# DeltaNet inverses: zeros above the diagonal written by GpSimd memsets, row and column factors in two bands

## The chip, the cores and the metric

The kernel runs on one core of a Trainium2 chip. The metric is the device time of one execution in microseconds, as the median of several runs. TensorE is called PE (its weight loads PEld), VectorE DVE, ScalarE ACT, GpSimd POOL and the queue of SyncE, which issues most transfers, SP.

## The reference

A linear-attention block (DeltaNet) feeds a mixture of experts. Batch 4, heads 8, sequence 768, head size 48; 3072 tokens of 384 numbers; 16 experts in 4 groups, hidden size 1024; everything in fp32.

```python
k_n = k / (np.linalg.norm(k, axis=-1, keepdims=True) + 1e-06)
for t in range(S):
    y[:, :, t] = q_t @ state
    v_old = state.T @ k_t
    state = state + beta_t * outer(k_t, v_t - v_old)
x = y.transpose(0, 2, 1, 3).reshape(B * S, H * D)
# one group by argmax, one expert in it by argmax, each token:
out = g_w * e_w * (relu(x @ w1[g, e]) @ w2[g, e])
```

(The middle lines are shortened to their meaning.)

## The kernel before

The sequence is cut into 24 chunks (u) of 32 steps. Inside a chunk the recurrence is a triangular system: with the products k·k of the chunk (gram, its products on line 253) and the factors beta/|k|^2 a unit lower triangular 32 x 32 matrix is inverted for every batch, head and chunk. Four chunks make a group (g, six of them). One group is 128 x 1024 numbers: on a partition lies one 32 x 32 matrix (tile m, 4 batches x 4 chunks x 8 heads = 128 matrices), and DVE inverts all 128 at once.

`inverse(g)` (from line 290 on) is that work. DVE turns the gram products into m (line 296). Square roots of the diagonal are made by DVE for group 0 and by POOL for the other groups (lines 307 to 312, 14 small steps on 128 x 32, result nrm); then r0 = -beta/|k|^2. Line 347 multiplies every row of m by its r0 (128 x 1024). Lines 355 to 383 run the elimination column by column, some 90 small DVE steps. Then line 386 builds cs, a table of -1 below the diagonal and 0 elsewhere (the constant `below`) times r0 by column, line 389 multiplies m by it, line 391 puts -r0 on the diagonal, and line 394 turns the result into mt. ACT spreads mt chunk by chunk into mtb (line 409, or 405 for the last group; each chunk two copies), the form that PE takes.

`advance(u)` is one chunk: PE adds vh (the values, scaled by DVE on line 435) and the old state's part into a_ps (lines 448, 454); ACT copies -a_ps to f (line 458); PE multiplies the inverse with it, w_ps from mtb and f (line 472); ACT copies w (line 475); PE updates the state s_ps (line 482), which ACT copies to s_bd (line 488); PE finishes the output o_ps (lines 496 or 501), which ACT copies to x (line 505). `logits(u)` turns x (t_ps, xt) and makes the router's logits (l_ps, lg); `route` does the routing per group partly on POOL, among it the comparisons `at` (line 602), whose products with `mine` PE adds up on line 684. Grams run ten chunks ahead.

The order of all engines in this stage is written out by hand. A loop over the chunks issues PE's and ACT's steps, and `work(n)` and `allow(...)` between them push the tasks that stand behind (the inverses, the routing): a task yields the size of each DVE step (or a word for what it waits for), `work` gives every task a credit and takes 100 plus that size from it per step:

```python
held[task] = said if isinstance(said, str) else None
due[task] -= 100 + (said if isinstance(said, int) else 0)
...
due[task] = min(due[task] + n * 180 * rate[task], 4000.0)
```

So the sizes that `inverse` yields decide between which steps of PE and ACT its own steps stand. The steps that it has on ACT (mtb) are issued when the task comes to ACT_STEP and SPREAD and the loop allows them. Each engine then runs its own list strictly in that order and waits by semaphores. After the attention the experts run one after the other, with weights of 3 MB each streamed in.

Constants (con) come in three loads: a small part, the table `below` (512 KB), and the rest. Before the first chunk PE multiplies columns of `below` by the identity into s_ps (line 787), products that nothing reads.

Of the kernel before, what the change touches and what calls it, by code (L numbers as in the profile page):

```python
# [8 lines left out]
F32 = mybir.dt.float32  # L9
I32 = mybir.dt.int32  # L10
AX = mybir.AxisListType
ALU = mybir.AluOpType
ACT = mybir.ActivationFunctionType
PSUM = bass.MemoryType.PSUM

C = 32
RG = 4
# [9 lines left out]
def constants(n_tokens, seq, n_experts, n_group, n_batch):  # L27
# [3 lines left out]
    p = np.arange(128)  # L31
    i, k = np.meshgrid(np.arange(C), np.arange(C), indexing="ij")
    u = np.arange(n_tokens // 128)
# [9 lines left out]
        "parity": np.stack([p // C % 2 == b2 for b2 in range(2)], axis=1),  # L43
        "below": np.tile(-(i > k).astype(np.float32).reshape(1, C * C), (128, 1)),
        "ident": (p[:, None] == p[None, :]),
# [13 lines left out]
    at, n = {}, 0  # L59
# [7 lines left out]
def deltanet_then_moe(  # L67
# [13 lines left out]
    nc = tc.nc  # L81
# [28 lines left out]
    con = cp.tile([128, const_d.shape[1]], F32, name="con")  # L110
    cut = {name: con[:, a:b] for name, (a, b) in const_at.items()}
    ident, before, ones = cut["ident"], cut["before"], cut["ones"]
# [64 lines left out]
    with ExitStack() as first:  # L177
# [21 lines left out]
        def load_kv(u):  # L199
            nc.sync.dma_start(out=kv_[u % NV], in_=kv_d[u])  # L200

        cols = [0, const_at["below"][0], const_at["ident"][0], const_d.shape[1]]

        def load_con(i):
            part = slice(cols[i], cols[i + 1])
            nc.sync.dma_start(out=con[:, part], in_=const_d[:, part])
# [13 lines left out]
        def of_kq(u, a=None):  # L220
            return (kqt_[u % NB][:, a or 0, 0], [lambda: load_kq(u, a)])
# [3 lines left out]
            RG: [of_kq(RG + 2), of_kq(RG + 3)],  # L225
            RG + 2: [of_kq(u, 1) for u in range(RG)] + [(cut["below"], [lambda: load_con(1)])],
            2 * RG: [(kv_[0], [lambda: load_kv(0), lambda: load_con(2), lambda: load_kv(1)])],
            2 * RG + 2: [of_kq(2 * RG), of_kq(2 * RG + 1)],
# [57 lines left out]
        def halves(g, uu):  # L286

            return range(1 if one_by_one(g, uu) else 2)

        def inverse(g):  # L290

# [4 lines left out]
            nc.vector.transpose(out=flat, in_=gts.pop(g).rearrange("p t u h -> p (t u h)"))  # L296
            yield C * C
            diag = flat[:, ::C + 1]
            nrm, r0, r1, r2 = [sm.tile([128, C], F32, tag=n, name=f"{n}{g}")
# [46 lines left out]
            yield FACTOR if g else 0  # L346
            nc.vector.tensor_tensor(m, m, r0[:, :, None].to_broadcast([128, C, C]), op=ALU.mult)  # L347
            yield C * C
            while g and g - 1 not in turned_over:
# [13 lines left out]
            for j in range(1, C - 1):  # L363
# [9 lines left out]
                else:  # L373
# [10 lines left out]
                    yield n * j  # L384
            cs = wk.tile([128, C, C], F32, tag="cs", name=f"cs{g}", bufs=1)
            nc.vector.tensor_tensor(cs, cut["below"].rearrange("p (i j) -> p i j", i=C),
                                    r0[:, None, :].to_broadcast([128, C, C]), op=ALU.mult)
            yield C * C
            nc.vector.tensor_tensor(m, m, cs, op=ALU.mult)
            yield C * C  # L390
            nc.vector.tensor_scalar(diag, r0, -1.0, None, op0=ALU.mult)
            yield
# [49 lines left out]
        def advance(u):  # L442
# [14 lines left out]
            f = wk.tile([128, H, D], F32, tag="f", name=f"f{u}")  # L457
            nc.scalar.activation(f, a_ps, ACT.Copy, scale=-1.0)
            o_ps = ps.tile([128, H, D], F32, tag="o", name=f"o_ps{u}")
# [295 lines left out]
        with tc.manual_schedule(engines={mybir.EngineType.PE, mybir.EngineType.DVE,  # L755
# [30 lines left out]
            for n in (H * D, H * D, H * D // 2):  # L786
                nc.tensor.matmul(s_ps[:, 0, 0:n], lhsT=ident, rhs=cut["below"][:, 0:n],
                                 start=True, stop=True, skip_group_check=True)
# [495 lines left out]
```

## Time and profile before

| | |
|---|---|
| median of the runs | 509.54 us (3 runs, 508.9 to 512.34) |
| profiled execution | 506.17 us, its span 504.4 us |
| granted TensorE clock, mean | 0.986 |
| PE busy | 465.6 us (92%) |
| DVE busy | 249.6 us (49%) |
| ACT busy | 187.3 us (37%) |
| POOL busy | 188.3 us (37%) |
| attention, up to the first expert product | 233.9 us of the span |

In the profile, "L347" is line 347. A row of a timeline has the start, the duration, engine, line, operation, output and inputs by the program's names, and in brackets the idle time of that engine just before and what ended it; `x32` means that many instructions merged, from the first start to the last end. Durations of neighbouring steps of one engine overlap by some 0.1 us, so a cost on the engine is better taken from start to start.

### The profile page before, as it was taken

Reading aid. Unit: us, or ns where it says so; the run is one execution under the profiler, and the core shown is the slowest. Engines: PE = TensorE matmul, PEld = TensorE weight load, DVE = VectorE, ACT = ScalarE, POOL = GpSimd, SP = SyncE. Lnnn points to the kernel's source line nnn. Section 1 sums busy time; section 2 is a strip of 40 time slices with the busy share of each in tenths; the row PEclk is TensorE's granted clock in tenths of the full one; section 3 lists DMA queues with packets and bytes.
Section 4 is the critical chain, followed back from the end, with each engine's and each line's share of the span. In section 5 each row is a group of like instructions: output and inputs, shape, how many; then the busy total and the mean of one; then the engine's idle time right before and its main releaser. Section 6 shows DMA issues by size and latency. Waiting matters only on the chain.

```text
span 504.4 us, 18596 instructions
## 1 busy us (share of the span) xinstructions
PE 465.6 (92%) x8012; PEld 428.2 (85%) x8012; DVE 249.6 (49%) x845; ACT 187.3 (37%) x396; POOL 188.3 (37%) x292
## 2 busy tenths in 40 slices
PE   3467999999999799899999999999999999999992
PEld 3345888878888688789999999999999999999992
DVE  2999999999999996528112012201201211012210
ACT  3224777677776667652121121112111111111110
POOL 0040110641715414010545454446525643356222
PEclk9997999999999999999999999999999999999997
DMA  5765445544435453221988779669868977789751
GB/s 181 228 223 167 142 152 172 156 134 155 146 104 168 139 170 109 71 64 36 289 279 275 254 223 302 221 202 324 269 190 276 323 270 218 245 298 303 229 182 40
DMA packets 57334, 99.98 MB, mean 198 GB/s; under 512 B 18974, under 2 KB 41433, under 8 KB 57251
## 3 DMA queue, kind: packets, MB, share of 16 engines
q1 hardware_dynamic: 51331, 88.77, 54.0%
q0 software_dynamic: 5920, 10.00, 6.5%
q8 instruction: 64, 1.05, 0.9%
q14 instruction: 19, 0.16, 0.1%
HBM read 84.63 MB, written 14.27 MB: 196 GB/s over the span
## 4 chain that ended last, share of the span: by engine, by line
PE 40%; DVE 29%; DMA 16%; issue 5%; POOL 4%; SPq 3%; ACT 2%; DVEq 0%; POOLq 0%; ACTq 0%
PE h_ps L1051 15%; PE y_ps L1070 14%; DMA y_dram<-yq 8%; DVE t L377 6%; DVE m L383 6%; DMA out_dram<-yo,to_i 5%; DVE m L360 4%; DMA yr<-y_dram 3%; SPq L1110 3%; PE w_ps L472 2%; DVE m L347 1%; DVE vh L435 1%; ACT s_bd L488 1%; DVE gqm L277 1%; PE x_ps L805 1%
## 5 line engine op out<-in xcount | busy, mean ns | idle before, releaser
L1070 PE MATMUL y_ps<-hid,w 128*128 128x224 f32 (+15 forms) x768 | 132.2, 332 | 0.0
L1070 PEld LDWEIGHTS y_ps<-hid,w 128*128 128x128 f32 x768 | 129.1, 190 | 0.3
L1051 PE MATMUL h_ps<-xt,w 128*128 128x232 f32 (+14 forms) x720 | 122.7, 330 | 0.0
L1051 PEld LDWEIGHTS h_ps<-xt,w 128*128 128x128 f32 x720 | 120.1, 190 | 0.3
L1023 POOL DMA_INDIRECT xq<-x_dram,from_q x92 | 87.6, 952 | 36.1 <-issue 24.7
L1054 ACT ACTIVATE hid<-h_ps 128x448 f32<-128x448 f32 (+15 forms) x64 | 32.1, 501 | 100.2 <-PE h_ps L1051 100.2
L1082 POOL DMA_INDIRECT out_dram<-yo,to_i x32 | 34.1, 1067 | 92.2 <-DVE yo L1120 82.3
L1073 DVE COPY yt<-y_ps 128x232 f32<-128x232 f32 (+13 forms) x14 | 5.1, 366 | 124.5 <-PE y_ps L1070 124.5
L1075 ACT ACTIVATE yt<-y_ps 128x224 f32<-128x224 f32 (+15 forms) x34 | 11.4, 336 | 116.6 <-PE y_ps L1070 116.6
L377 DVE TENSOR_TENSOR t<-m 128x81 f32<-128x81 f32 (+13 forms) x156 | 51.6, 331 | 0.2
L383 DVE TENSOR_TENSOR m<-m,t 128x81 f32<-128x81 f32 (+13 forms) x156 | 51.5, 330 | 0.0
L360 DVE SCALAR_TENSOR_TENSOR m<-m 128x29 f32<-128x29 f32 (+27 forms) x174 | 43.1, 251 | 0.4
L1120 DVE TENSOR_SCALAR yo<-yr,gate 128x384 f32<-128x384 f32 (+14 forms) x28 | 11.3, 422 | 61.4 <-DMA yr<-y_dram 51.6
L488 ACT ACTIVATE s_bd<-s_ps 48x768 f32<-48x768 f32 x46 | 37.0, 804 | 10.1 <-PE s_ps L482 9.5
L409 ACT ACTIVATE mtb<-mt,con 128x256 f32<-128x256 f32 x41 | 29.7, 737 | 4.2 <-DVE mt L394 4.2
L253 PE MATMUL g_ps<-kqt 48*32 48x64 f32 (+1 forms) x1216 | 18.4, 237 | 13.2 <-issue 8.5
L472 PE MATMUL w_ps<-f,mtb 64*64 64x48 f32 (+1 forms) x864 | 26.7, 217 | 2.5 <-ACT mtb L409 1.4
L472 PEld LDWEIGHTS w_ps<-f,mtb 64*64 64x64 f32 (+1 forms) x864 | 23.6, 128 | 5.8 <-issue 2.6
L454 PEld LDWEIGHTS a_ps<-s_bd,kqt 128*32 128x32 f32 x736 | 15.0, 110 | 15.9 <-ACT s_bd L488 7.2
L253 PEld LDWEIGHTS g_ps<-kqt 48*32 48x32 f32 x1216 | 14.4, 116 | 15.1 <-issue 9.4
L572 POOL TENSOR_TENSOR acc<-acc,hots 128x16 f32<-128x16 f32 x16 | 4.9, 307 | 57.3 <-DVE hots L570 56.3
L482 PE MATMUL s_ps<-w,kv 32*112 32x96 f32 x736 | 24.7, 272 | 0.0
(175 smaller groups left out, 589.2 us busy)
## 6 DMA issues: line engine op xcount, KB each, us to landing
w<-in_w_dram SPq DMA_DIRECT2D x29, 1536.0 KB, 12.1
kv<-in_kv_dram SPq DMA_DIRECT2D x24, 448.0 KB, 4.0
kqt<-in_kq_dram SPq DMA_DIRECT2D x20, 512.0 KB, 4.0
x_dram<-x SPq DMA_DIRECT2D x24, 192.0 KB, 2.1
w<-in_w_dram SPq DMA_DIRECT2D x24, 128.0 KB, 3.6
y_dram<-yq SPq DMA_DIRECT2D x36, 84.0 KB, 8.5
yr<-y_dram SPq DMA_DIRECT2D x14, 192.0 KB, 2.4
kqt<-in_kq_dram SPq DMA_DIRECT2D x8, 256.0 KB, 3.4
```

The source lines that it names most:

```text
L253: nc.tensor.matmul(g_out[quads[b], hh * NP + j, of], lhsT=kqt[rows, 0, j, quads[b]], rhs=kqt[rows, of, j, quads[b]], start=True, stop=True ...
L360: nc.vector.scalar_tensor_tensor(row, in0=m[:, j, 0:j], scalar=m[:, i, j:j + 1], in1=row, op0=ALU.mult, op1=ALU.add)
L377: nc.vector.tensor_tensor(tv, m[:, j + 2:, j:j + 1].to_broadcast([128, n, j]), m[:, j:j + 1, 0:j].to_broadcast([128, n, j]), op=ALU.mult)
L383: nc.vector.tensor_tensor(below, below, tv, op=ALU.add)
L409: nc.scalar.activation(mtb[:, rows, a], from_, ACT.Copy, scale=by)
L472: nc.tensor.matmul(w_ps[b, h], lhsT=mt[b, uu * H + (h % 2) * NP + h // 2], rhs=f[b, h], start=True, stop=True, skip_group_check=True)
L488: nc.scalar.activation(s_bd[rows, :, :, hh, :], s_at[rows, :, :, hh * D:(hh + 1) * D], ACT.Copy)
L1023: nc.gpsimd.indirect_dma_start(out=xq[:, g, :], out_offset=None, in_=x_dram[:, :].rearrange("n (q c) -> (n q) c", q=4), in_offset=bass.Ind ...
L1051: nc.tensor.matmul(h_ps[:, k], lhsT=w1[:, j, (f + k) * 128:(f + k + 1) * 128], rhs=xt[:, j, 0:R], start=(j == 0), stop=(j == DC - 1), skip ...
L1054: nc.scalar.activation(hid[:, f:f + 2], h_ps, ACT.Relu)
L1070: nc.tensor.matmul(y_ps, lhsT=w2[:, f, j * 128:(j + 1) * 128], rhs=hid[:, f], start=(f == 0), stop=(f == FC - 1))
L1082: put = nc.gpsimd.indirect_dma_start(out=out[:, :], out_offset=bass.IndirectOffsetOnAxis(ap=to[0:P, i:i + 1], axis=0), in_=yo[0:P, :], in_ ...
```

## The change

The constant `below` and its load go. Five memsets on POOL per group write zeros above the diagonal of m, right after DVE's turn: blocks of 16 x 16, then 2 of 8 x 8, 4 of 4 x 4, 8 of 2 x 2 and 16 single elements, slanted along the diagonal (496 elements per partition). The row factor is put on in two bands, rows 16 to 31 with all columns (512 elements) and rows 0 to 15 with columns 0 to 15 (256). The table cs is no longer built: m is multiplied by r0 by column in the same two bands, so without the -1 of `below`; the diagonal is a copy of r0 and not -r0, and f is a_ps instead of -a_ps, which takes the sign out. PE's unread products before the first chunk take columns of con from the identity on.

```diff
-        "below": np.tile(-(i > k).astype(np.float32).reshape(1, C * C), (128, 1)),
...
-        cols = [0, const_at["below"][0], const_at["ident"][0], const_d.shape[1]]
+        cols = [0, const_at["ident"][0], const_d.shape[1]]
...
-            RG + 2: [of_kq(u, 1) for u in range(RG)] + [(cut["below"], [lambda: load_con(1)])],
-            2 * RG: [(kv_[0], [lambda: load_kv(0), lambda: load_con(2), lambda: load_kv(1)])],
+            RG + 2: [of_kq(u, 1) for u in range(RG)],
+            2 * RG: [(kv_[0], [lambda: load_kv(0), lambda: load_con(1), lambda: load_kv(1)])],
...
+        bands = [(slice(C // 2, C), slice(0, C)), (slice(0, C // 2), slice(0, C // 2))]
...
             nc.vector.transpose(out=flat, in_=gts.pop(g).rearrange("p t u h -> p (t u h)"))
             yield C * C
+            n = C // 2
+            while n:
+                above = flat.rearrange("p (k q) -> p k q", q=64 * n)[:, :, 33 - 2 * n:33 + 31 * n]
+                nc.gpsimd.memset(above.rearrange("p k (i c) -> p k i c", c=C + 1)[:, :, :, 0:n], 0.0)
+                n //= 2
...
-            nc.vector.tensor_tensor(m, m, r0[:, :, None].to_broadcast([128, C, C]), op=ALU.mult)
-            yield C * C
+            for rows, cols in bands:
+                nc.vector.tensor_tensor(m[:, rows, cols], m[:, rows, cols],
+                                        r0[:, rows, None].to_broadcast([128, C // 2, cols.stop]),
+                                        op=ALU.mult)
+                yield C // 2 * cols.stop
...
-            cs = wk.tile([128, C, C], F32, tag="cs", name=f"cs{g}", bufs=1)
-            nc.vector.tensor_tensor(cs, cut["below"].rearrange("p (i j) -> p i j", i=C),
-                                    r0[:, None, :].to_broadcast([128, C, C]), op=ALU.mult)
-            yield C * C
-            nc.vector.tensor_tensor(m, m, cs, op=ALU.mult)
-            yield C * C
-            nc.vector.tensor_scalar(diag, r0, -1.0, None, op0=ALU.mult)
+            for rows, cols in bands:
+                nc.vector.tensor_tensor(m[:, rows, cols], m[:, rows, cols],
+                                        r0[:, None, cols].to_broadcast([128, C // 2, cols.stop]),
+                                        op=ALU.mult)
+                yield C // 2 * cols.stop
+            nc.vector.tensor_copy(diag, r0)
...
-            nc.scalar.activation(f, a_ps, ACT.Copy, scale=-1.0)
+            nc.scalar.activation(f, a_ps, ACT.Copy)
...
-                nc.tensor.matmul(s_ps[:, 0, 0:n], lhsT=ident, rhs=cut["below"][:, 0:n],
+                nc.tensor.matmul(s_ps[:, 0, 0:n], lhsT=ident, rhs=con[:, cols[1]:cols[1] + n],
```

PE's order stays as it was, row for row. The other engines' lists change as follows (a number behind a name is the chunk or the group, a number behind an underscore only names the buffer).

ACT's list at chunk 3, before (f3, w3 belong to chunk 3, xt2 and lg2 to the logits of chunk 2, mtb1 to group 1, whose first chunk is 4):

```order
L505 ACTIVATE x2_1360<-o_ps2_1217 128x384
L458 ACTIVATE f3_1398<-a_ps3_1380 128x384
L529 ACTIVATE xt2_1422<-t_ps2_1418 128x384
L475 ACTIVATE w3_1452<-w_ps3_1435 128x384
L258 ACTIVATE gt3_1272<-g_ps13_1454 128x8x32
L264 ACTIVATE gq13_1488<-g_ps13_1454 128x256
L488 ACTIVATE s_bd_99<-s_ps_103 48x16x48 x2
L535 ACTIVATE lg0_1020<-l_ps2_1508 128x20
L409 ACTIVATE mtb1_1370<-mt1_1368,con_66 128x8x32 x2
L505 ACTIVATE x3_1538<-o_ps3_1400 128x384
```

And the same place now:

```order
L513 ACTIVATE x2_1376<-o_ps2_1232 128x384
L417 ACTIVATE mtb1_1382<-mt1_1380,con_66 128x8x32 x2
L466 ACTIVATE f3_1413<-a_ps3_1395 128x384
L417 ACTIVATE mtb1_1382<-mt1_1380,con_66 128x8x32
L537 ACTIVATE xt2_1438<-t_ps2_1434 128x384
L417 ACTIVATE mtb1_1382<-mt1_1380,con_66 128x8x32
L483 ACTIVATE w3_1470<-w_ps3_1453 128x384
L257 ACTIVATE gt3_1287<-g_ps13_1472 128x8x32
L263 ACTIVATE gq13_1506<-g_ps13_1472 128x256
L496 ACTIVATE s_bd_99<-s_ps_103 48x16x48 x2
L543 ACTIVATE lg0_1031<-l_ps2_1526 128x20
L513 ACTIVATE x3_1555<-o_ps3_1415 128x384
```

The first pair of mtb1 has moved from behind lg2 to ahead of f3, and the second pair from behind f4 to behind f3. The first copy carries the wait for DVE's mt1. In the later groups the mtb copies stand where they stood.

DVE's list at the end of the second inverse and the beginning of the third, before:

```order
L386 TENSOR_TENSOR cs1_1363<-con_66,r01_773 128x1024
L389 TENSOR_TENSOR m1_766<-m1_766,cs1_1363 128x1024
L391 TENSOR_SCALAR m1_766<-r01_773 128x32
L337 RECIPROCAL r12_1162<-nrm2_1160 128x32
L394 STREAM_TRANSPOSE mt1_1368<-m1_766 128x1024
L339 TENSOR_TENSOR r12_1162<-r12_1162 128x32
L341 SCALAR_TENSOR_TENSOR r02_1161<-r12_1162,bt_98 128x32
L345 STREAM_TRANSPOSE normt2_1373<-nrm2_1160 128x32
L277 TENSOR_TENSOR gqm4_1378<-gq4_306,con_66 128x512
L347 TENSOR_TENSOR m2_1156<-m2_1156,r02_1161 128x1024
```

And now:

```order
L395 TENSOR_TENSOR m1_770<-m1_770,r01_783 128x512
L395 TENSOR_TENSOR m1_770<-m1_770,r01_783 128x16x16
L399 COPY m1_770<-r01_783 128x32
L402 STREAM_TRANSPOSE mt1_1380<-m1_770 128x1024
L343 RECIPROCAL r12_1177<-nrm2_1175 128x32
L345 TENSOR_TENSOR r12_1177<-r12_1177 128x32
L347 SCALAR_TENSOR_TENSOR r02_1176<-r12_1177,bt_98 128x32
L351 STREAM_TRANSPOSE normt2_1388<-nrm2_1175 128x32
L276 TENSOR_TENSOR gqm4_1393<-gq4_306,con_66 128x512
L354 TENSOR_TENSOR m2_1167<-m2_1167,r02_1176 128x512
L354 TENSOR_TENSOR m2_1167<-m2_1167,r02_1176 128x16x16
```

Two long steps have become two shorter ones at each factor, the table is gone, and the reciprocal that waits for POOL's nrm stands behind the turn mt1 and no longer ahead of it; in groups 3 and 4 it is the same.

POOL's list at the start of group 2's roots now (before, the roots followed nrm1 directly):

```order
L318 TENSOR_SCALAR nrm1_782<-r11_784 128x32
L302 MEMSET m2_1167 128x16x16
L302 MEMSET m2_1167 128x2x8x8
L302 MEMSET m2_1167 128x4x4x4
L302 MEMSET m2_1167 128x8x2x2
L302 MEMSET m2_1167 128x16
L313 TENSOR_TENSOR r22_1178<-r12_1177 128x32
```

The memsets stand ahead of the roots in POOL's queue and wait for DVE's turn of the same group; the roots wait for them by the queue alone. DVE waits for them by a semaphore only in group 0, at the first band of the row factor.

## Prediction

> **What bounds the kernel now.** I read the split by stage first (busy time of each engine in stretches cut where a row factor on DVE begins; the columns are stretch, length, then busy time and instructions of PE, PEld, DVE, ACT and POOL, granted clock, DMA share, GB/s).
>
> ```profile
> 10.30:42.90 32.60, 17.72 (x724) 12.65 (x707) 31.82 (x113) 9.26 (x32) 6.23 (x16) 1.00 0.61 212
> 42.90:72.10 29.20, 27.95 (x803) 22.97 (x797) 28.92 (x104) 20.47 (x41) 4.79 (x14) 0.88 0.49 155
> 72.10:102.90 30.80, 30.44 (x944) 25.36 (x942) 30.45 (x112) 22.76 (x45) 9.71 (x26) 1.00 0.48 151
> 102.90:135.10 32.20, 31.16 (x944) 26.14 (x942) 31.88 (x117) 22.93 (x47) 13.61 (x33) 1.00 0.45 149
> 135.10:166.60 31.50, 30.50 (x911) 25.48 (x907) 31.18 (x117) 21.93 (x44) 13.14 (x33) 1.00 0.45 138
> 166.60:195.00 28.40, 25.88 (x748) 21.42 (x751) 28.05 (x108) 19.44 (x37) 8.71 (x19) 1.00 0.49 149
> 234.00:504.00 270.00, 261.29 (x1563) 260.04 (x1561) 47.35 (x96) 43.86 (x99) 125.95 (x141) 0.99 0.76 245
> ```
>
> DVE is full from 10 to 195 us, and that is what the change relieves. But from 72 us on PE is full as well: 30.44 of 30.80, 31.16 of 32.20, 30.50 of 31.50. Time that DVE gives back there can be no more than the time for which PE waits. The experts (234 to 504) are PE's alone and untouched; a shift of the attention's end passes straight through. The second view is PE's waits between 72 and 235 us (total, times, longest):
>
> ```profile
> PE a_ps L454 <- ACT s_bd L488: 2.1, 6, 1.3
> PE s_ps L684 <- POOL at L602: 1.3, 2, 0.9
> PE a_ps L448 <- DVE vh L435: 1.2, 2, 0.8
> ```
>
> That is all that a faster DVE can win there: POOL's `at` is late because DVE's `what` is late, `vh` is DVE's own, and the one long wait on s_bd is this, in the timelines of ACT and PE:
>
> ```profile
> 165.62 1.38 ACT L409 ACTIVATE mtb<-mt,con 128x256 f32<-128x256 f32 x2 [1.18 <-DVE mt L394]
> 166.90 1.62 ACT L488 ACTIVATE s_bd<-s_ps 48x768 f32<-48x768 f32 x2
> 168.57 0.87 PE L454 MATMUL a_ps<-s_bd,kqt 128*32 128x96 f32 x32 [1.32 <-ACT s_bd L488]
> ```
>
> ACT stands at the copy of a turned inverse (mtb) until DVE has turned it (mt), and everything behind it in ACT's queue, here the state s_bd that PE needs, stands with it. That row is the model for what I expect below.
>
> **The change, part by part.** *DVE.* Durations are taken start to start, from DVE's timeline where the second inverse ends and the third begins:
>
> ```profile
> 67.06 1.22 DVE L386 TENSOR_TENSOR cs<-con,r 128x1024 f32<-128x1024 f32 x1
> 68.32 1.22 DVE L389 TENSOR_TENSOR m<-m,cs 128x1024 f32<-128x1024 f32 x1
> 69.58 0.20 DVE L391 TENSOR_SCALAR m<-r 128x32 f32<-128x32 f32 x1
> 69.67 0.34 DVE L337 RECIPROCAL r<-nrm 128x32 f32<-128x32 f32 x1
> 69.93 1.19 DVE L394 STREAM_TRANSPOSE mt<-m 128x1024 f32<-128x1024 f32 x1
> 71.47 0.65 DVE L277 TENSOR_TENSOR gqm<-gq,con 128x512 f32<-128x512 f32 x1
> 72.03 1.22 DVE L347 TENSOR_TENSOR m<-m,r 128x1024 f32<-128x1024 f32 x1
> 73.28 0.77 DVE L355 SCALAR_TENSOR_TENSOR m<-m 128x30 f32<-128x30 f32 x3
> 195.34 0.41 DVE L273 TENSOR_TENSOR gqm<-gq,con 128x256 f32<-128x256 f32 x1
> ```
>
> The table of column factors (L386) costs 68.32 - 67.06 = 1.26 us and goes. A 1024-element product costs 1.25 (L347) or 1.26 (L389). A band of 512 is like gqm at 71.47: 72.03 - 71.47 = 0.56; one of 256 like the row at 195.34, 0.41 less the 0.09 by which 71.47's 0.65 exceeds its 0.56: 0.32. With 0.04 for the wait behind the second band, two bands are 0.92 and save 0.33 twice. The diagonal stays 0.2 as a copy. Per group 1.26 + 0.66 = 1.9 us; over six groups 11.5 us of DVE. Bounds: no gain from bands (1.26 a group) to exactly three quarters (1.26 + 0.63).
>
> *POOL.* Five memsets of 256, 128, 64, 32 and 16 elements per partition ahead of the roots. The nearest rows are memsets of 72 and 12 elements:
>
> ```profile
> 253.07 0.18 POOL L1061 MEMSET yt<- 128x72 f32 x1
> 255.05 0.11 POOL L1061 MEMSET yt<- 128x12 f32 x1 [1.80 <-DVE yq L1106]
> 98.75 1.12 POOL L312 TENSOR_SCALAR nrm<-r 128x32 f32<-128x32 f32 x1
> 10.33 1.25 DVE L296 STREAM_TRANSPOSE m<-gt 128x1024 f32<-128x1024 f32 x1 [7.84 <-ACT gt L258]
> 14.63 1.22 DVE L347 TENSOR_TENSOR m<-m,r 128x1024 f32<-128x1024 f32 x1
> ```
>
> Sixty elements cost 0.07, so 1.2 ns each and 0.095 to begin: 496 elements in five are 0.6 + 0.5 = 1.1 us. The upper bound is the third row, a POOL step held 1.12 us while DVE runs its 1024-element product: 5 x 1.12 = 5.6. I take 1.1, as DVE's steps are short where the memsets run. They delay nrm, for which DVE's reciprocal waits, but the 1024-element products that stretch nrm's last two steps go too, and DVE arrives with a lead: no cost. In the first group the row factor waits for the memsets, with DVE's own root work from 11.6 (10.33 + 1.25) to 14.6, 3 us, as cover; without it 1.1 us.
>
> [...]
>
> *The order of the work.* The tasks pay for each step by its size, so the second inverse now ends earlier in the written order, and its first copies on ACT (mtb1) move from behind lg of chunk 2 to ahead of f of chunk 3: six of ACT's waits for PE earlier, nearly one whole chunk. PE's order is unchanged. DVE does not become that much earlier. ACT before, then PE:
>
> ```profile
> 64.22 0.49 ACT L505 ACTIVATE x<-o_ps 128x384 f32<-128x384 f32 x1
> 65.88 0.49 ACT L458 ACTIVATE f<-a_ps 128x384 f32<-128x384 f32 x1 [1.17 <-PE a_ps L454]
> 71.64 1.39 ACT L409 ACTIVATE mtb<-mt,con 128x256 f32<-128x256 f32 x2
> 66.40 0.55 PE L523 MATMUL t_ps<-con,x 128*128 128x128 f32 x3
> 66.88 1.14 PE L472 MATMUL w_ps<-f,mtb 64*64 64x48 f32 x32
> 68.73 1.04 PE L482 MATMUL s_ps<-w,kv 32*112 32x96 f32 x32
> ```
>
> By then DVE has saved two groups, 3.8 us, and 0.1 for the reciprocal now behind mt: mt1 ends at 69.93 + 1.19 - 3.9 = 67.2. ACT comes to the pair at about 64.7 and waits, 1.35 more for the pair, and f of chunk 3 starts at 68.6 instead of 65.88. PE's w_ps follows f by 0.5: 69.1 against 66.88. Two more copies and xt (0.7, 0.4, 0.7) lie between f and w: s_ps at 71.3 against 68.73. **Stall: +2.6 us** on the path, whatever PE wins at the start. There it waits 1.39 us for the first group's mtb (first row of the next fence), which DVE now gives 1.9 sooner; PE beginning 1.4 to 1.9 sooner only makes the wait at chunk 3 longer. PE is then idle from 65.5 (66.88 - 1.4) or earlier to 69.1, 3.6 us or more.
>
> What idleness does to PE is seen at the start, where it paused 1.39 us before 41.36 and 1.25 before 44.39 (PE's rows, then the clock by stretches, in the column before the last two):
>
> ```profile
> 41.36 1.13 PE L472 MATMUL w_ps<-f,mtb 64*64 64x48 f32 x32 [1.39 <-ACT mtb L409]
> 44.39 0.48 PE L253 MATMUL g_ps<-kqt 48*32 48x64 f32 x17 [1.25 <-issue]
> 44.80 1.82 PE L482 MATMUL s_ps<-w,kv 32*112 32x96 f32 x32
> 50.00 0.87 PE L454 MATMUL a_ps<-s_bd,kqt 128*32 128x96 f32 x32
> 43.00:44.00 1.00, 0.14 (x12) 0.00 (x0) 1.00 (x1) 0.22 (x3) 0.00 (x0) 0.58 0.00 0
> 49.00:50.00 1.00, 1.00 (x2) 0.00 (x1) 1.00 (x6) 1.00 (x3) 0.00 (x0) 0.50 0.39 151
> 50.00:51.00 1.00, 1.00 (x49) 1.00 (x52) 1.00 (x6) 0.36 (x2) 0.00 (x0) 1.00 0.46 164
> ```
>
> The clock was halved until 50.0, s_ps took 1.82 instead of 1.04, and of the 5.2 us from 44.8 to 50.0 half, 2.6, was lost. The pause at chunk 3 is longer. Its cost lies between nothing and 2.6; part of the slow work hides in w's own wait for ACT, and I take **+1.5**.
>
> [...]
>
> *Won back later.* From chunk 4 on PE is late and DVE early, some 8 us apart, so DVE waits for PE's grams rather than PE for DVE. `at`: -1.3. The pair of `vh` and s_bd: at 168.57 ACT's pair could start 1.2 sooner, -1.2, and the second `vh` wait of 0.8 leaves 0.2 for s_bd (the five short ones are (2.1 - 1.3) / 5 = 0.16), -0.6. Together **-3.1**. Not recovered: the five short waits for s_bd, which belong to each chunk.
>
> *Costing nothing:* the 512 KB of table no longer loaded, its marker on ACT and its place in SP's queue: DVE, full from 10 us on, waits for no load in that stretch. The sign moved into f, the copy for the diagonal, and the warm-up products on other numbers keep their sizes.
>
> **Sum:** +2.6 + 1.5 - 3.1 = +1.0 us. The profiled execution took 506.17, with 1.77 around its span of 504.4; it becomes 507.2. The median of the runs shown is 509.54, 3.37 above it, and becomes 510.5.
>
> **Rivals.** (1) *DVE's saving passes.* If the pair does not hold f, or holds it for less, PE starts 1.4 to 1.9 us sooner and still wins the 3.1 back: 5 us, 504.5, and with part of its clock loss at the start avoided too, 502; with all of DVE's 11.5 it would be 498. For it: DVE's nearly unbroken busyness and the long DVE stretches in the chain that ended last. Against: PE's 30.44 of 30.80, and ACT's written order. (2) *PE stays cold*: slower. If the pause of chunk 3, with the waits for w behind it, keeps the clock halved for 6 us and more, as from 43 to 50, the loss is 2.6 to 4, and if it cools again at a later wait 2.6 more: +2.6 + 4 - 3.1 = +3.5, 513, up to 515.5. It decides from about 3 us of halved clock on. For it: the rows above; against: the long runs at 1.00 after 50 us, with waits of up to 1.3. (3) *The bands save nothing*, each paying its own start: mt1 1.3 later, the stall 3.9, the rest as forecast: 512. Against: 0.56 for 512 elements.
>
> **How the numbers follow.** Forecast 0.60, rival 1 0.16, rival 2 0.15, rival 3 0.09. One per cent, 5.1 us, is about what a measurement of this kernel tells from no change. Rival 1 passes that bound in most of its outcomes (0.12), rival 2 in its upper part (0.09), and the rest lies within: 0.79. The range reaches to rival 1's 504.5 and rival 2's 515.5.
>
> **What would show it.** Right: ACT's first pair of mtb1 waits for DVE's mt by 2 to 4 us around 65 to 68; PE idle 3 to 6 us ahead of w_ps of chunk 3, clock about 0.5 behind it; no more waits of PE on `at` and `vh` after 100 us; DVE about 11 us less busy, with idle time in the later groups; L386 gone, bands near 0.56 and 0.32; memsets near 1.1 us a group. Wrong: no wait at mtb1, or an attention stage that ends 5 us earlier, or DVE waiting for POOL's memsets.

## The result and the profile after

The changed kernel took 515.23 us (median of 4 runs, 514.12 to 517.16) beside 509.25 for the kernel before on the same chip (4 runs): ratio 1.0103, 95% interval 1.006 to 1.0147. Six later runs on another chip gave 1.0085 (1.0067 to 1.0102). So it is about one per cent slower: the forecast's 510.5 was 4.7 us low, the time lies 0.3 us inside the upper end of the range (515.5), and it lies on the bound of one per cent at which I had parted "same" from "slower". The profiled execution took 515.33 us with a span of 513.6 (before 506.17 and 504.4); the mean granted clock fell from 0.986 to 0.978.

Line numbers shift by the change: row bands are L354, column bands L395, the diagonal's copy L399, mt L402, mtb L417, vh L443, a_ps L456 and L462, f L466, w_ps L480, s_ps L490.

First ACT's timeline of the changed kernel around chunk 3 (start, duration, what, idle time before and its releaser):

```profile
60.68 0.49 ACT L513 ACTIVATE x<-o_ps 128x384 f32<-128x384 f32 x1
68.77 1.37 ACT L417 ACTIVATE mtb<-mt,con 128x256 f32<-128x256 f32 x2 [7.59 <-DVE mt L402]
70.03 0.48 ACT L466 ACTIVATE f<-a_ps 128x384 f32<-128x384 f32 x1
```

ACT does nothing from 61.2 to 68.77, and f of chunk 3, which stands behind the pair in its list and whose a_ps is ready at 63.1 (first row of the next fence), starts at 70.03 instead of 65.88. PE's timeline of the same execution:

```profile
62.20 0.87 PE L462 MATMUL a_ps<-s_bd,kqt 128*32 128x96 f32 x32
63.66 0.55 PE L531 MATMUL t_ps<-con,x 128*128 128x128 f32 x3
70.56 1.95 PE L480 MATMUL w_ps<-f,mtb 64*64 64x48 f32 x32 [6.35 <-ACT f L466]
73.55 1.82 PE L490 MATMUL s_ps<-w,kv 32*112 32x96 f32 x32
78.58 1.65 PE L456 MATMUL a_ps<-vh,con 128*128 128x384 f32 x2
80.15 1.51 PE L462 MATMUL a_ps<-s_bd,kqt 128*32 128x96 f32 x32
82.80 1.14 PE L480 MATMUL w_ps<-f,mtb 64*64 64x48 f32 x32
```

PE idles 6.35 us, and then works at a granted clock of 0.50: w_ps takes 1.95 instead of 1.14 (the last row), s_ps 1.82 instead of 1.04. The split by short stretches has the granted clock in the column before the last two:

```profile
72.00:73.00 1.00, 1.00 (x52) 0.91 (x55) 1.00 (x7) 0.60 (x2) 0.00 (x0) 0.50 0.00 0
80.00:81.00 1.00, 1.00 (x25) 0.85 (x28) 1.00 (x6) 0.00 (x0) 0.00 (x0) 0.50 0.54 197
81.00:82.00 1.00, 1.00 (x44) 1.00 (x36) 1.00 (x5) 0.27 (x1) 0.00 (x0) 0.66 0.00 0
82.00:83.00 1.00, 1.00 (x29) 0.69 (x22) 1.00 (x5) 0.95 (x3) 0.00 (x0) 1.00 0.00 0
```

PE is fully busy there, and the clock is half until about 81.7 (0.66 as the mean of 81 to 82 is half a clock for two thirds of it), 11 us after the pause ended. What was to be won back shows in PE's waits from 72 to 235 us (total, times, longest):

```profile
PE a_ps L462 <- ACT s_bd L496: 1.4, 7, 0.5
PE o_ps L509 <- issue: 1.3, 3, 0.5
PE g_ps L252 <- issue: 0.5, 1, 0.5
```

The waits on `at` and `vh` are gone and the long one on s_bd too. The table sets the executions beside each other. It has the start of the first w product of a chunk in PE's timeline, the first expert product and the span, all in us, and the time's ratio to the kernel before, measured beside it; e1 to e12 are the experiments of the next section. A set is what ran on one chip, with the kernel before beside it: the kernel before took 510.54 us (median of 7) in set 1, 504.75 (11) in set 2, 505.26 (13) in set 3.

| kernel | set | chunk 0 | 1 | 3 | 4 | 20 | experts | span | ratio (95%) |
|---|---|---|---|---|---|---|---|---|---|
| before | 0 | 41.36 | 51.94 | 66.88 | 74.73 | 199.44 | 233.85 | 504.4 | 1 |
| changed | 0 | 40.39 | 47.35 | 70.56 | 82.80 | 204.72 | 241.84 | 513.6 | 1.0103 (1.0060 to 1.0147) |
| e1_old_yields | 1 | 39.68 | 46.51 | 63.24 | 71.25 | 193.26 | 230.78 | 504.0 | 0.9858 (0.9819 to 0.9896) |
| e2_new_yields_alone | 1 | 41.29 | 53.37 | 73.09 | 84.93 | 206.17 | 243.08 | 514.9 | 1.0175 (1.0128 to 1.0222) |
| e3_memsets_alone | 1 | 41.32 | 52.87 | 67.81 | 75.67 | 201.09 | 237.90 | 510.3 | 1.0072 (1.0055 to 1.0088) |
| e4_filled_pause | 1 | 40.96 | 48.05 | 71.02 | 78.48 | 199.00 | 237.50 | 509.5 | 1.0072 (1.0056 to 1.0089) |
| e5_dead_load | 2 | 40.98 | 49.96 | 65.65 | 73.53 | 194.66 | 227.70 | 497.8 | 0.9923 (0.9907 to 0.9939) |
| e6_change_again | 2 | 40.23 | 47.06 | 70.59 | 82.47 | 203.17 | 236.21 | 506.4 | 1.0085 (1.0067 to 1.0102) |
| e7_memsets_behind_roots | 2 | 40.71 | 47.54 | 64.24 | 72.14 | 193.56 | 226.60 | 496.7 | 0.9917 (0.9890 to 0.9944) |
| e8_before_again | 2 | 41.97 | 53.02 | 67.95 | 75.80 | 200.09 | 233.12 | 504.1 | 1 |
| e9_pause_filled_more | 3 | 40.79 | 47.62 | 72.86 | 80.33 | 201.27 | 236.06 | 506.2 | 1.0052 (1.0032 to 1.0071) |
| e10_spreads_behind_f | 3 | 41.00 | 48.38 | 63.89 | 71.75 | 194.06 | 227.10 | 497.2 | 0.9878 (0.9858 to 0.9897) |
| e11_both | 3 | 40.25 | 47.11 | 65.43 | 73.31 | 195.31 | 228.36 | 498.4 | 0.9903 (0.9884 to 0.9921) |
| e12_old_yields_again | 3 | 39.96 | 50.99 | 65.94 | 73.84 | 195.36 | 228.40 | 498.5 | 0.9890 (0.9866 to 0.9914) |

How to read it: from chunk 20 to the experts every execution of sets 2 and 3 takes 33.0 us (e9 34.8), but the first pair 34.4 and 37.1, and set 1 36.8 to 38.5, whatever the kernel; the rest behind it is 270 to 271 us in sets 2 and 3 and 272 to 273 in set 1. So the 2.7 + 1.2 us of the 9.2 by which the first two spans differ behind chunk 20 are not put down to the change: in e6 and e8, the same two kernels, that part is 33.0 us each and then 270.2 and 271.0. Chunk 20 is the place to compare, and there the change costs 5.3 us (first pair) or 3.1 (e6 and e8).

### The profile page after: what moved, and what is told of

Same layout as the page of the kernel before. It is cut to its first block, busy times and chain, and to the rows that moved or that the text cites. A ratio compares the mean times of both kernels' runs of the same rounds, so it can differ in the third digit from the quotient of the medians.

```text
span 513.6 us, 18628 instructions
## 1 busy us (share of the span) xinstructions
PE 470.7 (92%) x8012; PEld 432.1 (84%) x8012; DVE 243.6 (47%) x851; ACT 186.7 (36%) x395; POOL 184.8 (36%) x322
## 4 chain that ended last, share of the span: by engine, by line
PE 69%; DMA 11%; DVE 8%; ACT 5%; issue 4%; POOL 1%; SPq 1%; DVEq 0%; POOLq 0%; ACTq 0%
PE y_ps L1078 18%; PE h_ps L1059 18%; DMA out_dram<-yo,to_i 6%; PE w_ps L480 5%; PE s_ps L490 5%; PE a_ps L462 3%; PE l_ps L436 3%; ACT s_bd L496 3%; DMA y_dram<-yq 3%; PE o_ps L471 3%; PE o_ps L504 3%; PE a_ps L456 2%; PE g_ps L252 2%; PE t_ps L531 2%; DMA yr<-y_dram 2%
## 5 line engine op out<-in xcount | busy, mean ns | idle before, releaser
L386 DVE TENSOR_TENSOR t<-m 128x81 f32<-128x81 f32 (+13 forms) x156 | 53.7, 344 | 0.3
L496 ACT ACTIVATE s_bd<-s_ps 48x768 f32<-48x768 f32 x46 | 37.0, 804 | 14.4 <-PE s_ps L490 10.7
L480 PE MATMUL w_ps<-f,mtb 64*64 64x48 f32 (+1 forms) x864 | 27.7, 220 | 7.3 <-ACT f L466 6.4
L480 PEld LDWEIGHTS w_ps<-f,mtb 64*64 64x64 f32 (+1 forms) x864 | 24.5, 132 | 10.8 <-ACT f L466 6.9
L417 ACT ACTIVATE mtb<-mt,con 128x256 f32<-128x256 f32 x41 | 29.9, 743 | 9.7 <-DVE mt L402 9.7
L462 PEld LDWEIGHTS a_ps<-s_bd,kqt 128*32 128x32 f32 x736 | 15.8, 114 | 15.5 <-ACT s_bd L496 6.8
L580 POOL TENSOR_TENSOR acc<-acc,hots 128x16 f32<-128x16 f32 x16 | 5.5, 341 | 63.1 <-DVE hots L578 62.1
L252 PE MATMUL g_ps<-kqt 48*32 48x64 f32 (+1 forms) x1216 | 18.4, 240 | 10.4 <-issue 5.3
L490 PE MATMUL s_ps<-w,kv 32*112 32x96 f32 x736 | 25.5, 273 | 0.9 <-issue 0.8
L456 PE MATMUL a_ps<-vh,con 128*128 128x384 f32 x48 | 24.1, 587 | 0.9 <-DVE vh L443 0.7
```

The costliest lines, as they stand in the source:

```text
L386: nc.vector.tensor_tensor(tv, m[:, j + 2:, j:j + 1].to_broadcast([128, n, j]), m[:, j:j + 1, 0:j].to_broadcast([128, n, j]), op=ALU.mult)
L456: nc.tensor.matmul(a_ps.rearrange("p h d -> p (h d)"), lhsT=ident, rhs=vh.rearrange("p h d -> p (h d)"), start=True, stop=(u == 0), skip_g ...
L480: nc.tensor.matmul(w_ps[b, h], lhsT=mt[b, uu * H + (h % 2) * NP + h // 2], rhs=f[b, h], start=True, stop=True, skip_group_check=True)
L490: nc.tensor.matmul(s_at[0:KR, b, j], lhsT=k[quads[b], j, 0:KR], rhs=w[quads[b], 2 * j:2 * j + 2], start=(u == 0 and j == 0), stop=True, sk ...
L496: nc.scalar.activation(s_bd[rows, :, :, hh, :], s_at[rows, :, :, hh * D:(hh + 1) * D], ACT.Copy)
```

## The experiments

Theory: the new step sizes moved the first two spreads of group 1 ahead of chunk 3's f in ACT's list, ACT waits there for DVE, PE idles, its clock drops; the work that the change saves is real, but lies behind this. Rivals: the memsets and the bands themselves cost the time (DVE's operation on the diagonal takes 0.77 and 0.52 us beside the memsets in groups 0 and 2, before 0.19 and 0.18); or the clock, not the list, is the whole of it.

**1. The change with the old order.** The sizes that a task reports are put back, nothing else:

```diff
             for rows, cols in bands:
                 nc.vector.tensor_tensor(m[:, rows, cols], m[:, rows, cols],
                                         r0[:, rows, None].to_broadcast([128, C // 2, cols.stop]),
                                         op=ALU.mult)
-                yield C // 2 * cols.stop
+            yield C * C
...
                                         r0[:, None, cols].to_broadcast([128, C // 2, cols.stop]),
                                         op=ALU.mult)
-                yield C // 2 * cols.stop
+                yield C * C
```

> The changed kernel whole, but the factor steps report the sizes of before to the planner (one report of 1024 after both row bands, 1024 after each column band), so that PE's and ACT's lists are those of the kernel before, but for ACT's tag operation of the dropped load. Order theory (the 6 us come from ACT's list, in which the first two spreads of group 1 now stand ahead of chunk 3's f): no pause of PE ahead of chunk 3's w, w of chunk 3 at 62 to 64 us (before 66.9, less the 3.5 to 4.6 that chunk 2 had already gained), the at and vh waits of PE shorter, and a time of 498 to 505, that is 1 to 2% faster than before. Rival 1 (the five memsets and the bands cost the time, by holding up DVE): the time stays near 515. Rival 2 (the gain of the early chunks is due to the new order too): 507 to 510, as before.

504.08 us, 0.9858. No pause ahead of chunk 3, its w at 63.24. As the order theory has it; the first rival falls: with the memsets and the bands, but the old list, the kernel is 1.4% faster than before. The second rival is not tested here, since pause and low clock go together; experiment 4 parts them. DVE's list is the old one too, so that ACT's list alone is not yet shown to be the cause (experiment 10).

**2. The new order with the old work.** The converse: the kernel before with the new sizes.

```diff
             nc.vector.tensor_tensor(m, m, r0[:, :, None].to_broadcast([128, C, C]), op=ALU.mult)
-            yield C * C
+            yield C // 2 * C
+            yield C // 2 * C // 2
...
                                     r0[:, None, :].to_broadcast([128, C, C]), op=ALU.mult)
-            yield C * C
+            yield C // 2 * C
             nc.vector.tensor_tensor(m, m, cs, op=ALU.mult)
-            yield C * C
+            yield C // 2 * C // 2
```

> The kernel before with all of its old work (the column-factor table, full products, no memsets), but with reports of the new sizes to the planner (512 and 256 after the row product, 512 after the table, 256 after the column product), so that PE's and ACT's lists are those of the changed kernel. Order theory: DVE's mt of group 1 comes at about 71 us as before, ACT waits for it ahead of chunk 3's f, PE idles 8 to 9 us and then runs on the low clock for some 10 us; w of chunk 3 at 72 to 73.5, and a time of 518 to 522 (before + 5.5 to 6.5 stall + 4.4 cold + part won back). Rival (the order alone is harmless, the memsets and bands cost): 507 to 511.

517.8 us, 1.0175: the order alone, of ACT and DVE, costs 1.75% (1.3 to 2.2). Its ACT, and then its PE:

```profile
71.30 1.36 ACT L410 ACTIVATE mtb<-mt,con 128x256 f32<-128x256 f32 x2 [5.12 <-DVE mt L395]
72.57 0.47 ACT L459 ACTIVATE f<-a_ps 128x384 f32<-128x384 f32 x1
```

```profile
73.09 1.82 PE L473 MATMUL w_ps<-f,mtb 64*64 64x48 f32 x32 [4.67 <-ACT f L459]
75.95 1.82 PE L483 MATMUL s_ps<-w,kv 32*112 32x96 f32 x32
84.93 1.14 PE L473 MATMUL w_ps<-f,mtb 64*64 64x48 f32 x32
```

f and w fall where expected, set by the end of mt. The pause is 4.67 us and not 8 to 9, since PE itself is later here, and the time just under the 518 to 522. From chunk 3 to chunk 4 the clock costs as much as behind 6.35 us: 84.93 - 73.09 = 11.84.

**3. The memsets alone**, in the kernel before, ahead of the line `diag = flat[:, ::C + 1]`:

```diff
+            n = C // 2
+            while n:
+                above = flat.rearrange("p (k q) -> p k q", q=64 * n)[:, :, 33 - 2 * n:33 + 31 * n]
+                nc.gpsimd.memset(above.rearrange("p k (i c) -> p k i c", c=C + 1)[:, :, :, 0:n], 0.0)
+                n //= 2
```

> The kernel before with the five memsets added in each group, all else (the table with its mask, full products, orders of PE, ACT and DVE) as before; the mask makes the zeros superfluous, the result is the same. [...] Rival (memsets hold up DVE more than the trace of the change shows): 512 or more.

513.86 us, 1.0072: the rival's number, 3.7 us. Had the memsets cost no more than the trace of the change shows of them, it would have been 509 to 511 by my estimate. The trace locates less: chunk 20 is 1.0 to 1.65 us later than in the two profiles of before. The memsets do what they did in the change: 0.67 us of POOL for the five, and DVE's operation on the diagonal takes 0.77 us instead of 0.19. PE's wait for the first mtb is 2.5 us, and its clock drops behind it (w_ps of chunk 0 takes 1.56 instead of 1.13, s_ps 1.82 instead of 1.04). Where the rest of the 3.7 us arises I did not find; set 1 has no profile of the kernel before.

```profile
10.97 0.77 DVE L320 TENSOR_SCALAR r<-m 128x32 int32<-128x32 int32 x1
11.00 0.67 POOL L301 MEMSET m<- 128x256 f32 x5 [10.54 <-DVE m L296]
41.32 1.56 PE L477 MATMUL w_ps<-f,mtb 64*64 64x48 f32 x32 [2.50 <-ACT mtb L414]
```

**4. The change with PE kept busy** in the pause: products into o_ps, which the next product overwrites.

```diff
             o_ps = ps.tile([128, H, D], F32, tag="o", name=f"o_ps{u}")
+            for _ in range(10 if u == 3 else 0):
+                nc.tensor.matmul(o_ps.rearrange("p h d -> p (h d)"), lhsT=ident,
+                                 rhs=con[:, cols[1]:cols[1] + H * D], start=True, stop=True,
+                                 skip_group_check=True)
```

> The changed kernel with ten more 128x384 products of the identity (into o of chunk 3, which the next product overwrites) set ahead of chunk 3's o products, so that PE is busy for some 4.5 to 5 us of its 6.35 us pause. Theory (of the loss 4.4 us are the low clock behind the pause): w of chunk 3 still at 70.6, but its products and those up to 81 us at full clock, w of chunk 4 at 78 to 79 rather than 82.8, and a time of 510.5 to 512.5. Rival (the low clock costs little at the end, because later waits swallow it): 514 to 516. If the pause of 1.5 us that is left is enough to lower the clock, the same 514 to 516 with low-clock rows in the trace.

513.73 us, 1.0072. PE's timeline:

```profile
63.10 6.72 PE L469 MATMUL o_ps<-con 128*128 128x384 f32 x20
71.02 1.14 PE L484 MATMUL w_ps<-f,mtb 64*64 64x48 f32 x32
72.87 1.04 PE L494 MATMUL s_ps<-w,kv 32*112 32x96 f32 x32
78.48 1.14 PE L484 MATMUL w_ps<-f,mtb 64*64 64x48 f32 x32
```

Chunk 3's work takes what it takes at a whole clock (w_ps 1.14, s_ps 1.04): 78.48 - 71.02 = 7.46 us to chunk 4 where the change takes 82.80 - 70.56 = 12.24, and chunk 4 begins 4.0 to 4.3 us sooner, as the theory says. The ten products take 6.72 us and not 4.5 to 5, so that nothing is left of the pause and w of chunk 3 begins 0.4 to 0.5 us later than in the change. The time lies between the theory's 510.5 to 512.5 and the rival's 514 to 516, and by the ratios it is only 0.1 to 0.3% under the change, which is nearer the rival. So the low clock is not the whole of it: with the clock whole the kernel is still 0.7% slower than before. The profiled execution (511.34) is the fastest of the five (511.34 to 514.19), so that its trace may flatter it.

**5. The table still loaded**, nothing using it; otherwise as experiment 1. PE has a gap of 1.25 us in chunk 0's grams before (43.1 to 44.4) and none after, and I wanted to know whether the dropped load is why.

```diff
+        "below": np.tile(-(i > k).astype(np.float32).reshape(1, C * C), (128, 1)),
...
-            RG + 2: [of_kq(u, 1) for u in range(RG)],
+            RG + 2: [of_kq(u, 1) for u in range(RG)] + [(cut["below"], [lambda: load_con(1)])],
```

> The changed kernel with the old reports (as e1_old_yields), but the table of the mask, which nothing uses any more, is still loaded (512 KB, at its old place behind the key loads of the first four chunks). Load theory (the dropped load is why PE has no gap in chunk 0's grams at about 43 us and keeps its clock there): the gap of 0.6 to 1.4 us and the low clock at 44 to 50 come back, w of chunk 1 at 50 to 52 rather than 46.5, and a time of 507 to 509. Rival (the half microsecond that DVE saves ahead of the first spread does it): w of chunk 1 at 46 to 47.5, and a time of 502 to 505 as without the load.

500.38 us, 0.9923. Neither expectation holds whole. The gap is back in PE's timeline, but the clock stays; w of chunk 1 is at 49.96 all the same, after a second gap of 0.85 us:

```profile
42.44 0.71 PE L253 MATMUL g_ps<-kqt 48*32 48x64 f32 x47
43.67 0.35 PE L253 MATMUL g_ps<-kqt 48*32 48x64 f32 x17 [0.52 <-issue]
43.95 1.04 PE L491 MATMUL s_ps<-w,kv 32*112 32x96 f32 x32
```

Of the fourteen profiles the five with the load have this gap and the nine without it have not. By time the load is worth nothing that can be measured: 0.9923 beside 0.9917 for experiment 7 in the same set, whose memsets stand elsewhere but which has no load.

**6. The change and 8. the kernel before, once more**, unaltered, for second profiles.

> The changed kernel unaltered, for a second profile and a closer time, beside which the kernel with the filled pause (513.7) stands. If the low clock behind the pause is worth what its trace says (4.3 us) and the rest agrees, 516 to 518; if later waits swallow part of it, 514 to 516. The pause of 6 to 6.5 us ahead of chunk 3's w recurs in either case. At the tail of the recurrence (o products of chunk 22): if the three gaps of 0.4 to 0.5 us and the low clock behind them belong to the program, they are here again; if they are chance, not.

> The kernel before unaltered, for a second profile: the first one, at 506.2 us, lies under nearly all its timed runs (509 to 512). If the three gaps in chunk 22's o products and the low clock behind them belong to every kernel here and were only missing in that one execution, they are in this one, chunk 23's w comes 10 to 11 us after chunk 22's rather than 6.4, and the execution takes 509 to 511; if they come from the change, they are not here. The gap in chunk 0's grams at 43 us with the low clock behind it should be here either way, if it belongs to the program.

508.91 us and 1.0085; 505.89 us. The pause is 6.35 us again and w of chunk 3 at 70.59. The gap in chunk 0's grams is there in the kernel before (1.25 us), with s_ps at 1.82 us instead of 1.04 behind it. The three gaps in chunk 22's o products are in neither, nor in any profile of this set. They were in the first profile of the change and in all four of set 1, with the memsets and without, so they do not belong to the change.

**7. The memsets behind POOL's roots**, otherwise as experiment 1: the loop of memsets stands as clear() behind the last step that makes nrm (for group 0 behind DVE's first step).

```diff
                 nc.gpsimd.tensor_scalar(nrm, r1, -1.0, -1e-6, op0=ALU.mult, op1=ALU.add)
+                clear()
                 yield ROOTS
```

> The changed kernel with the old reports (as e1_old_yields), and in each group the memsets behind POOL's roots rather than ahead of them, so that POOL begins the roots 0.67 us earlier and DVE's first operation on the diagonal no longer runs beside the memsets. Contention theory (the memsets cost 0.3 to 0.5 us of DVE per group and 0.67 us of POOL in the chain that ends in the row factor; both partly hidden): the 0.52 to 0.77 us of that DVE operation fall to 0.2, and the time is 501 to 504, up to 3 us under e1_old_yields. Rival (DVE's waits there are hidden by its other work): 503 to 505, no difference.

499.98 us, 0.9917. DVE's operation on the diagonal falls to 0.17 to 0.19 us in groups 1 to 5 (group 0, where the memsets stand right behind this step in the program: 0.77). The time is no better than that of the same kernel with the memsets in front (0.9890 in experiment 12, in another set): hidden, as the rival has it. The operation of groups 1 to 5 in the changed kernel and then here (shortest, median and longest duration in ns, first and last start):

```profile
L310 DVE TENSOR_SCALAR r<-m x5: 180/297/661, 33.0 to 159.2; 128x32 int32<-128x32 int32 x5
L313 DVE TENSOR_SCALAR r<-m x5: 171/174/191, 33.1 to 152.0; 128x32 int32<-128x32 int32 x5
```

**9. The pause filled further**, thirteen products for ten.

> As e4_filled_pause with thirteen products instead of ten, so that PE is busy for some 5.9 of the 6.35 us: the low clock behind the pause should be gone, the pause itself stays. Theory (the low clock is worth 4 us at the end): 0.7 to 0.9% under the changed kernel's ratio of 1.0085 to 1.0103, that is a ratio of 1.000 to 1.003. Rival (about half of it or more is swallowed by later waits, as the 1.0072 of e4_filled_pause says): 1.005 to 1.009.

508.11 us, 1.0052. The thirteen take 8.65 us in PE's timeline, more than the pause, and push chunk 3 back:

```profile
63.01 8.65 PE L469 MATMUL o_ps<-con 128*128 128x384 f32 x26
72.86 1.13 PE L484 MATMUL w_ps<-f,mtb 64*64 64x48 f32 x32
80.33 1.14 PE L484 MATMUL w_ps<-f,mtb 64*64 64x48 f32 x32
```

So the kernel doesn't test what it was meant to. It pays 2.3 us at chunk 3 and takes 7.47 from there to chunk 4 instead of 11.88: 2.1 us sooner at chunk 4, and 1.7 us less by the ratios (1.0085 - 1.0052, uncertain by 1.3). So most of what it wins at chunk 4 seems to be there at the end, with bounds of 0.4 to 3.0 us.

**10. One step of waiting for group 1's spreads.** This alters ACT's list alone: the lists of PE and DVE are word for word those of the changed kernel.

```diff
+            if g == 1:
+                yield NEXT
             yield ACT_STEP
```

> The changed kernel whole, its new reports too, with one more step of waiting for group 1 ahead of its spreads, so that they stand behind chunk 3's f as before: the lists of PE and DVE are word for word those of the changed kernel, and ACT's list alone differs. Order theory in its narrow form (it is ACT's list, not DVE's new order): no pause ahead of chunk 3's w, w of chunk 3 at 62.5 to 64.5 us, and a ratio to before of 0.985 to 0.993, as e1_old_yields and e7_memsets_behind_roots had. Rival (DVE's new order is what costs, by late vh or masks): 1.000 or more, with the pause moved to another wait.

499.0 us, 0.9878 (0.9858 to 0.9897): the narrow form of the theory. ACT's timeline, where f now stands ahead of the pair:

```profile
62.89 0.49 ACT L468 ACTIVATE f<-a_ps 128x384 f32<-128x384 f32 x1 [1.25 <-PE a_ps L464]
68.57 0.19 ACT L545 ACTIVATE lg<-l_ps 128x20 f32<-128x20 f32 x1
68.65 1.39 ACT L417 ACTIVATE mtb<-mt,con 128x256 f32<-128x256 f32 x2
```

PE's, w of chunks 3 and 4:

```profile
63.89 1.14 PE L482 MATMUL w_ps<-f,mtb 64*64 64x48 f32 x32
71.75 1.13 PE L482 MATMUL w_ps<-f,mtb 64*64 64x48 f32 x32
```

The pair starts at 68.65, within 0.12 us of where the changed kernel had it, and waits for nothing: nobody needs it sooner. Against the changed kernel chunk 3 begins 6.7 us earlier, chunk 4 10.7, the experts 9.1 (beside e6), and by the two ratios the time is 2.07% (uncertain by 0.26) or 10.4 us (1.3) less, from one added wait.

**11. Both**, experiment 10 with the memsets behind the roots, and **12. experiment 1 again**, on the same chip.

> e10_spreads_behind_f with the memsets behind POOL's roots as well (the candidate for the best version). If the memsets' place is hidden: within 0.2% of e10_spreads_behind_f. If their 0.45 us of DVE and 0.67 us of POOL per group reach the path: 0.3 to 0.6% under it.

> e1_old_yields unaltered, on the same chip as e10 and e11, since its first ratio of 0.986 stands beside 0.992 for the nearly equal e7_memsets_behind_roots on another chip. If the memsets' place is hidden and the difference is the chip's: within 0.3% of e11_both. If DVE's new order is of use by itself, e10_spreads_behind_f is 0.3% or more under this one.

500.38 us, 0.9903, and 500.26, 0.9890. The memsets' new place does not help; 0.25% over experiment 10, if anything it costs. Experiment 12 shows that with the old list for DVE too the gain is the same within the intervals. Experiment 10 has the lowest median of set 3, 1.2% under the kernel before and 2.1% under the change; experiments 1, 11 and 12 cannot be told from it by their intervals.

## Why the prediction was right, and where it was not

*The mechanism* was as put: not DVE's work but ACT's list decides. ACT waits at the pair, f of chunk 3 stands behind it, PE pauses, its clock drops, and part is won back between chunks 4 and 20. Experiments 2 and 10 show it from both sides. The sizes were not: the time rose by 6.0 and 4.2 us and not by 1.0. That 515.23 still lies within the range is luck in part. The end of the range, 515.5, stands for a second drop of the clock at a later wait; here one drop, of 4.4 us and not 1.5, and a stall of 3.7 reached as far.

*The wait on ACT* was foreseen as 2 to 4 us and is 7.59, as PE, and with it ACT, came through chunks 0 to 2 faster (chunk 1 at 47.35 instead of 51.94), and as mt1 came 1.5 us later than forecast. The faster start does not move f, as the prediction says of PE's gain at the start; f hangs on mt. PE idles 6.35 us, just above the 3 to 6 foreseen.

*Stall, +2.6.* The prediction took this at s_ps; for w of chunk 3 its numbers say 69.1 - 66.88 = +2.2. Measured there: +3.7 (first pair) and +2.6 (e6 less e8, where before itself was 1.1 later). The model for f (end of mt, 1.35 for the pair, 0.5 to w) held to 0.1 us; the end of mt did not, 68.74 instead of 67.2. DVE had saved 2.4 us by then and not 3.9. DVE's timeline of the changed kernel has both reasons (the operation on the diagonal of groups 0 and 2, the row bands of group 0, mt1), and behind it stand the same two operations before:

```profile
11.56 0.77 DVE L321 TENSOR_SCALAR r<-m 128x32 int32<-128x32 int32 x1
15.23 1.03 DVE L354 TENSOR_TENSOR m<-m,r 128x512 f32<-128x512 f32 x2
16.29 0.78 DVE L364 SCALAR_TENSOR_TENSOR m<-m 128x30 f32<-128x30 f32 x3
58.91 0.52 DVE L310 TENSOR_SCALAR r<-m 128x32 int32<-128x32 int32 x1
67.49 1.25 DVE L402 STREAM_TRANSPOSE mt<-m 128x1024 f32<-128x1024 f32 x1
```

```profile
11.61 0.19 DVE L315 TENSOR_SCALAR r<-m 128x32 int32<-128x32 int32 x1
59.94 0.18 DVE L304 TENSOR_SCALAR r<-m 128x32 int32<-128x32 int32 x1
```

Two bands cost 16.29 - 15.23 = 1.06 us and not 0.92; whether the second start or the shorter rows cost it, no run parts. Four pairs before mt1: 0.6 us. And the first operation on the diagonal takes 0.77 and 0.52 beside the memsets, where it took 0.19 and 0.18: 0.9 us. Together the 1.5 missing. The prediction's "no cost" for the memsets looked only at POOL's side and at the row factor. It also overstated their own time, 1.1 us:

```profile
11.59 0.67 POOL L302 MEMSET m<- 128x256 f32 x5 [11.13 <-DVE m L297]
58.93 0.68 POOL L302 MEMSET m<- 128x256 f32 x5 [20.48 <-DVE m L297]
```

The operation on the diagonal ends at 12.33, just behind the memsets' 12.26. Beside the memsets it takes 0.77 and 0.52 us instead of 0.19 and 0.18. It starts 0.03 and 0.02 us ahead of them, and in group 2 it ends at 59.43, ahead of the memsets' 59.61. What holds it up there no run shows.

*Clock, +1.5 within 0 to 2.6.* This term, an estimate from the drop of the clock at the start of the kernel before, failed. From chunk 3 to chunk 4 the change takes 12.24 and 11.88 us, with a whole clock 7.85 (before) and 7.86 (experiment 10): 4.0 to 4.4 us (0.4 more beside the 7.46 of experiment 4). The step at fault is "part of the slow work hides in w's own wait for ACT": there is no such wait, PE is the bound for all of the 11 us. The upper bound was wrong as well, since it took the length of the first drop of the clock for the length of any. By the end this term is not fully settled: experiment 10, with 10.4 us (1.3) for 6.7 of stall and 4.0 of clock, says that most of it arrives, and so does experiment 9 with 1.7 (1.3) for 2.1 at chunk 4; experiment 4 says that 0.7 to 1.6 does.

*Won back, -3.1.* From chunk 4 to chunk 20 before takes 124.71 and 124.29 us, the change 121.92 and 120.70: 2.8 and 3.6. The size was right. But experiment 2, with all of DVE's old work, takes 121.24 there: PE's lateness by itself wins this back. Without it the saving wins 2.2 (experiment 10: 122.31), so the two do not add up.

*DVE, 11.5 us less* was too much: DVE is busy 243.6 us instead of 249.6. Of the 5.5 us that are missing the bands make 1.7 (0.14 us twelve times) and the operation on the diagonal about 1.6 over six groups; the rest is not located.

*The sum.* With the measured sizes it is 3.7 + 4.4 - 2.8 = +5.3 (first pair) or 2.6 + 4.0 - 3.6 = +3.0 (second) instead of +1.0, and the times say +6.0 and +4.2. That is the stretch of rival 2 (+3.5, up to +6), to which I gave 0.15: "halved for 6 us and more" is what happened. "Within one per cent", to which I gave 0.79, stands and falls with its edge: 1.03% and 0.85%. Rival 1, the saving passing, is what happens once the list is mended: its 504.5 to 498 beside 503.3, which is the 509.54 of the forecast times experiment 10's 0.9878. Of the 5.4 and 6.0 us that experiment 10 gains at chunk 20 on the two profiles of before, 3.0 and 4.1 are there at chunk 3 already (63.89 instead of 66.88 and 67.95), from a start in which the clock does not drop (s_ps of chunk 0 takes 1.04 us). Rival 3 was half true: a band pair saves 0.19 of 1.25 us, not 0.33 and not nothing.

*Costing nothing.* The dropped load: right by the time, though PE's gap in chunk 0 goes with it. The memsets: not right, 0.7% alone in the kernel before, of which the trace explains less than half. Whether the change pays this too no run shows: experiments 7 and 11 move the memsets and do not take them away.

## What to carry to other kernels

Where a planner is fed with step sizes, a smaller size is a change of the program's order: set the lists of every engine before and after side by side, and ask of each step that moved forward whether its input is there by then and who stands behind it. Here the pair that waited cost little (in experiment 10 it starts within 0.12 us of the same time, and the kernel is 2.07% faster); f of chunk 3, queued behind it, came 4.15 us later (70.03 instead of 65.88), and the pause of PE was paid again in the clock, 4.0 to 4.4 us by chunk 4. If the list got worse, hold back the one step before giving up the edit: here that turned +0.9% into -1.2%.

## What the runs showed of the hardware that I had not expected

- After a pause of 6.35 us PE ran at a granted clock of 0.50 for 11 us without an idle moment (70.6 to 81.7). After 4.67 us (experiment 2) it was slow for about as long: from w_ps at 73.09, 1.82 us instead of 1.14, to a_ps at 82.55, 1.31 instead of 0.87. In the kernel before, behind waits of 1.39 and 1.25 us, the clock was halved for some 6 us (until 50.0).
- The length of the pause alone did not settle whether the clock dropped: a wait of 1.22 us for the first mtb left it whole (e1), one of 1.49 in the very same kernel (e12) did not, and chunk 1 began 4.5 us later; in experiment 2 the products right behind a wait of 1.78 ran at a whole clock (w_ps 1.13 us). The profile's clock column still says 1.00 in e12 (second row below); the durations of the products tell. PE's timeline of e1, a stretch and PE's timeline of e12, and PE's of experiment 2:

```profile
39.68 1.14 PE L480 MATMUL w_ps<-f,mtb 64*64 64x48 f32 x32 [1.22 <-ACT mtb L417]
40.00:41.00 1.00, 1.00 (x20) 1.00 (x22) 0.97 (x4) 0.00 (x0) 0.00 (x0) 1.00 0.05 21
39.96 1.94 PE L480 MATMUL w_ps<-f,mtb 64*64 64x48 f32 x32 [1.49 <-ACT mtb L417]
42.94 1.82 PE L490 MATMUL s_ps<-w,kv 32*112 32x96 f32 x32
50.99 1.14 PE L480 MATMUL w_ps<-f,mtb 64*64 64x48 f32 x32
41.29 1.13 PE L473 MATMUL w_ps<-f,mtb 64*64 64x48 f32 x32 [1.78 <-ACT mtb L410]
```

- By chunk 20 half of that is left (e12 is 2.1 us behind e1 there), and the intervals of their ratios overlap.
- Beside POOL's memsets DVE's operation on 32 numbers per partition took 0.58 us longer in group 0 (0.77 instead of 0.19), with the memsets alone added too (experiment 3); where the memsets were moved away from it, it took 0.17 to 0.19 (experiment 7, groups 1 to 5).
- Three gaps of 0.35 to 0.47 us in chunk 22's products, with slower products behind them (a_ps 1.65 us instead of 0.91 in the changed kernel), come and go between sets of runs of the same kernel and are worth over 3 us in the span. A single profile of each kernel would have put them down to the change.
